# One head per 64-row matmul: splitting the product of v_m and w1 into two row halves, two banks and 32-partition evictions

## The chip, the cores and the metric

The kernel runs as one program on one core of a Trainium2 chip. The metric is the device time of one execution in microseconds (us); lower is better. The engines are named as the profile names them: PE (matmul), PEld (the weight loads of PE), DVE (VectorE), ACT (ScalarE), POOL (GpSimd) and SP (the queue that issues DMAs). A "column" of a matmul below is one column of its moving operand.

## What is computed

```python
# q, k, v: (8 batches, 8 heads, 576, 64); phi: (8, 8, 576, 32)
a = softmax(phi, axis=2)                       # over the 576 positions
k_m = einsum('bhsm,bhsd->bhmd', a, k)          # 32 memory rows per head
v_m = einsum('bhsm,bhsd->bhmd', a, v)
attn = softmax(q @ k_m.T / 8, axis=-1)         # over the 32 memory rows
x = concat_heads(attn @ v_m)                   # (4608, 512)
p = domain_probs / domain_probs.sum(-1)        # (4608, 4)
for e in range(4):                             # w1[e]: 512 x 1024, w2[e]: 1024 x 512
    out += p[:, e:e+1] * (relu(x @ w1[e]) @ w2[e])
```

## The kernel before

**The folding.** `x @ w1` is never formed from `x`. Since `x` is `attn @ v_m`, the kernel first multiplies each head's `v_m` (32 x 64) by that head's 64 rows of `w1`; this product is called `vw`. Then the first expert product takes `vw` and the transposed attention `AT`, and contracts over 8 heads x 32 memory rows = 256 instead of 512.

**Numbers.** Nearly every operand is held as a high part, rounded to fp32r, and a low part that is the rest. A product is three matmuls: high by high, high by low, low by high. So every eviction from PSUM that makes such an operand is a pair: ACT copies (and thereby rounds) the high part, then DVE subtracts it from the PSUM value for the low part.

**The stages.** The eight batches are taken as four pairs `k`; each pair has `PAIR = 128` steps, 32 for each of the four experts `e`. A step `s` stands for one batch of the pair (`odd`), one half of its 576 positions and one `j` of the eight 128-wide slices of the 1024 hidden columns. In step `s` the loop at L628 to L631 does three things: it runs the units that a plan has put at `s`, it issues `first(s + 2)` and it issues `second(s)`.

- `first` (L405) makes six matmuls (L415 to L417, twice) of 256 or 320 columns into a tile `p1`, then the relu on ACT (L427) and the low part on DVE (L429) into `h`, and for the wide halves into `hm` too.
- `second` (L434) makes six matmuls of 512 columns (L445 to L447, twice; nine where the middle tile is due) into `p2` tiles, and at the last `j` adds them into `acc` on DVE (L460, L462).

**The part that is changed.** `vw_unit` (L392) makes `vw` for one pair of heads `hp` and one half `fh` of the hidden columns. It calls `vw_mm` (L361): three matmuls of 512 columns (L364 to L366) into one PSUM tile `pv` of 128 partitions x 512. The stationary operand is `vt`, written by `write_vt` (L281): its 128 rows are the 64 dimensions of the two heads of the pair, its 128 columns are four blocks of 32 (two batches x two heads), and it is zero where row and column are not of the same head. So one product gives both heads of both batches. `vw_out` (L369) then evicts, for each batch in `odds`, 64 partitions: one ACT copy (L379) and one DVE subtraction (L380).

**Where the units stand.** The eight units of an expert are planned in the steps 26 to 33 (`VW_AT`) counted from the start of the expert before it, one in each step, both batches each. There are 15 such windows. The first expert of the first pair is made apart: four units by `vw_mm` in the prologue, which the change doesn't touch, four units for the even batch and eight for the odd batch within the first 18 steps, one batch each. That makes 120 + 12 = 132 units by `vw_unit`. Beside the units, the same windows hold the splits of the next expert's weights (L118 on ACT, L119 on DVE).

**PSUM and the order of work.** There are eight PSUM tiles: four with the tag `p2` for the sums of `second`, and four with the tag `pm`, which everything else takes in turn: `p1`, `pv` and the tiles of the attention. A tile with the tag `pm` can be taken again once all reads of the tile four allocations earlier are done. After the prologue, which is scheduled by hand, a scheduler puts the instructions of each engine into one fixed order; each engine then runs its list in that order and waits where an operand isn't there.

Of the kernel before, what the change touches and what calls it, by code (L numbers as in the profile page):

```python
# [28 lines left out]
F32 = mybir.dt.float32  # L29
F32R = mybir.dt.float32r  # L30
# [5 lines left out]
B, H, S, D, M = 8, 8, 576, 64, 32  # L36
N, DM, E, F = 4608, 512, 4, 1024
P = 128
# [31 lines left out]
def body(ctx: ExitStack, tc: tile.TileContext, qm, qt, kv, kvt, phi, prob, w1, w2, out):  # L70
    nc = tc.nc
    pool = lambda name, **k: ctx.enter_context(tc.tile_pool(name=name, bufs=1, **k))
    const, wp, work, att = pool("const"), pool("wp"), pool("work"), pool("att")
    psum = pool("psum", space=PSUM)
# [40 lines left out]
    w1t, w2t = {}, {}  # L115
# [25 lines left out]
    st = {}  # L141
# [217 lines left out]
    vw = {}  # L359

    def vw_mm(k, fh, hp, tag):  # L361
        vt, w = st["vt", k], w1t[fh, hp]
        ps = psum.tile([P, 512], F32, name="pv", tag=tag[0], bufs=tag[1])
        nc.tensor.matmul(ps, vt[:, hp, 0, :], w[:, 0, :], start=True, stop=False)  # L364
        nc.tensor.matmul(ps, vt[:, hp, 0, :], w[:, 1, :], start=False, stop=False)  # L365
        nc.tensor.matmul(ps, vt[:, hp, 1, :], w[:, 0, :], start=False, stop=True)  # L366
        return ps

    def vw_out(ps, fh, hp, odds):  # L369
        g = hp // 2  # L370
        for odd in odds:
            if hp % 2 == 0:
                vw[odd, fh, g] = att.tile(
                    [P, 2, 512], F32R, name="vw", tag=f"vw{odd}", bufs=4 + odd
                )
            q = (hp % 2) ^ odd
            r = slice(64 * q, 64 * q + 64)
            t = vw[odd, fh, g]
            nc.scalar.copy(t[r, 0, :], ps[r])  # L379
            nc.vector.tensor_sub(t[r, 1, :], ps[r], t[r, 0, :].bitcast(F32))  # L380
# [9 lines left out]
        nc.gpsimd.tensor_sub(t[r, 1, :], tmp[r, 0, :], t[r, 0, :].bitcast(F32))  # L390

    def vw_unit(k, e, fh, hp, odds, tag):  # L392
        vw_out(vw_mm(k, fh, hp, tag), fh, hp, odds)


    hs, mid, acc, po = {}, {}, {}, {}
# [83 lines left out]
    def vw_at(s, *a):  # L480
        at(s, lambda: vw_unit(*a, ("pm", 4)))

    rest = [unit_scores(0, t0) for t0 in (2, 4)] + [lambda t0=t0: transposes(0, t0) for t0 in (2, 4)]
    rest += [unit_w1(0, 0, 1, g) for g in range(2)]
    rest += [unit_w2(0, 0, j2) for j2 in range(1, 4)]
    rest += [lambda hp=hp: vw_unit(0, 0, 1, hp, (0,), ("pm", 4)) for hp in range(NP)]
    for s, u in zip(REST_0, rest):
        at(s, u)
# [9 lines left out]
    for k in range(NG):  # L498
        for e in range(E):
            s = k * PAIR + e * STEPS  # L500
            nk, ne = (k, e + 1) if e + 1 < E else (k + 1, 0)
            if nk < NG:
                for j2 in range(4):
                    at(s + W2_AT[j2], unit_w2(nk, ne, j2))
                n = 0
# [6 lines left out]
        if k + 1 < NG:  # L512
            b = 2 * k + 2
# [37 lines left out]
    with tc.manual_schedule():  # L551
# [45 lines left out]
        q = raw["qm", 0, 0]  # L597
# [9 lines left out]
        for i in range(2):  # L607
            t = wp.tile([P, 2, DM], F32R, name="w2", tag="w2", bufs=NJ + 2)
# [3 lines left out]
        for i in range(2):  # L612
            t = w2t[0, 0, i]
            dve.tensor_sub(t[:, 1, :], raw["w2", 0, 0][:, i, :], t[:, 0, :].bitcast(F32))
        pv = [vw_mm(0, 0, hp, ("p2", 4)) for hp in range(4)]
# [52 lines left out]
```

## Time and profile before

| what | value |
|---|---|
| time, median of 2 runs | 1426.86 us (1426.07 to 1427.65) |
| time of the profiled execution | 1428.84 us |
| its span, first to last instruction | 1427.1 us |
| PE busy | 1412.3 us (99%), 7808 matmuls |
| PEld busy | 1233.5 us (86%) |
| DVE busy | 837.2 us (59%), 1853 instructions |
| ACT busy | 620.2 us (43%), 1543 instructions |
| POOL busy | 27.8 us (2%) |
| mean granted TensorE clock | 0.996 |

How to read it: a matmul's listed duration runs from its start to its modelled end, and matmuls overlap, so a 512-column matmul that lasts 0.39 us in the list can be followed by the next one 0.23 us later. What a matmul costs is the distance from its start to the start of the next. DVE and ACT instructions that follow each other without a wait overlap a little as well. Idle time of an engine that nothing waits for costs nothing.

### The profile page before, as it was taken

Reading aid. Unit: us, or ns where it says so; the run is one execution under the profiler, and the core shown is the slowest. Engines: PE = TensorE matmul, PEld = TensorE weight load, DVE = VectorE, ACT = ScalarE, POOL = GpSimd, SP = SyncE. Lnnn points to the kernel's source line nnn. Section 1 sums busy time; section 2 is a strip of 40 time slices with the busy share of each in tenths; the row PEclk is TensorE's granted clock in tenths of the full one; section 3 lists DMA queues with packets and bytes.
Section 4 is the critical chain, followed back from the end, with each engine's and each line's share of the span. In section 5 each row is a group of like instructions: output and inputs, shape, how many; then the busy total and the mean of one; then the engine's idle time right before and its main releaser. Section 6 shows DMA issues by size and latency. Waiting matters only on the chain.

```text
span 1427.1 us, 20830 instructions
## 1 busy us (share of the span) xinstructions
PE 1412.3 (99%) x7808; PEld 1233.5 (86%) x7808; DVE 837.2 (59%) x1853; ACT 620.2 (43%) x1543; POOL 27.8 (2%) x27
## 2 busy tenths in 40 slices
PE   7999999999999999999999999999999999999998
PEld 6888888888888888888888888888888888888887
DVE  7876638666385654837547375573846446272722
ACT  6655426453263533635335362452625234161521
POOL 3300000000000000000000000000000000000000
PEclk8999999999999999999999999999999999999999
DMA  6632303323141120412214121140323103030001
GB/s 245 198 118 75 121 28 126 104 64 104 39 161 61 64 89 16 137 58 78 94 63 135 59 88 65 46 130 18 107 75 96 60 25 94 1 119 1 1 30 38
DMA packets 35957, 115.20 MB, mean 81 GB/s; under 512 B 3984, under 2 KB 5136, under 8 KB 35856
## 3 DMA queue, kind: packets, MB, share of 16 engines
q1 hardware_dynamic: 35856, 113.86, 24.5%
q8 instruction: 62, 1.02, 0.3%
q14 instruction: 39, 0.32, 0.1%
HBM read 104.41 MB, written 9.44 MB: 80 GB/s over the span
## 4 chain that ended last, share of the span: by engine, by line
PE 92%; DMA 2%; DVE 2%; ACT 2%; issue 1%; POOL 0%; SPq 0%; ACTq 0%
PE p L446 18%; PE p L447 18%; PE p L445 18%; PE p L415 9%; PE p L417 9%; PE p L416 9%; PE sc L304 2%; PE pv L366 2%; PE pv L364 2%; PE x L230 2%; PE pv L365 2%; DMA stage<-in_w 1%; PE tp L349 1%; PE kvp L249 1%; ACT w L118 0%
## 5 line engine op out<-in xcount | busy, mean ns | idle before, releaser
L446 PE MATMUL p<-w,h 128*128 128x512 f32 x1024 | 404.3, 395 | 0.0
L447 PE MATMUL p<-w,h 128*128 128x512 f32 x1024 | 402.8, 394 | 0.0
L445 PE MATMUL p<-w,h 128*128 128x512 f32 x1024 | 402.7, 393 | 0.0
L427 ACT ACTIVATE h<-p 128x256 fp32r<-128x256 f32 x512 | 195.2, 382 | 331.5 <-PE p L417 294.3
L429 DVE SCALAR_TENSOR_TENSOR h<-p,h 128x256 fp32r<-128x256 f32 x512 | 213.9, 418 | 206.3 <-ACT h L427 110.0
L415 PE MATMUL p<-AT,vw 128*128 128x256 f32 (+1 forms) x1024 | 308.2, 301 | 0.0
L417 PE MATMUL p<-AT,vw 128*128 128x256 f32 (+1 forms) x1024 | 304.3, 297 | 0.1
L416 PE MATMUL p<-AT,vw 128*128 128x256 f32 (+1 forms) x1024 | 303.6, 297 | 0.0
L447 PEld LDWEIGHTS p<-w,h 128*128 128x128 f32 x1024 | 192.4, 188 | 43.3 <-DVE nm L154 0.2
L119 DVE TENSOR_TENSOR w<-stage,w 128x512 fp32r<-128x512 f32 x259 | 175.9, 687 | 78.4 <-ACT w L118 77.1
L445 PEld LDWEIGHTS p<-w,h 128*128 128x128 f32 x1024 | 193.2, 189 | 23.3
L446 PEld LDWEIGHTS p<-w,h 128*128 128x128 f32 x1024 | 192.6, 188 | 22.0
L416 PEld LDWEIGHTS p<-AT,vw 128*128 128x128 f32 x1024 | 194.5, 190 | 19.5 <-DVE AT L356 0.3
L415 PEld LDWEIGHTS p<-AT,vw 128*128 128x128 f32 x1024 | 194.0, 189 | 19.1
L417 PEld LDWEIGHTS p<-AT,vw 128*128 128x128 f32 x1024 | 193.5, 189 | 0.7 <-DVE vw L380 0.6
L118 ACT CAST w<-stage 128x512 fp32r<-128x512 f32 x262 | 159.6, 620 | 79.1 <-DMA stage<-in_w 47.3
L380 DVE TENSOR_TENSOR vw<-pv,vw 64x512 fp32r<-64x512 f32 x254 | 172.1, 685 | 8.9 <-ACT vw L379 5.5
L429 DVE SCALAR_TENSOR_TENSOR hm<-p,hm 128x64 fp32r<-128x64 f32 x256 | 56.0, 219 | 201.9 <-ACT h L427 200.9
L379 ACT CAST vw<-pv 64x512 fp32r<-64x512 f32 x254 | 145.5, 580 | 58.5 <-DVE vw L380 42.6
L427 ACT ACTIVATE hm<-p 128x64 fp32r<-128x64 f32 x256 | 56.6, 221 | 227.9 <-PE p L417 227.9
L462 DVE SCALAR_TENSOR_TENSOR acc<-p,pt,acc 128x512 f32<-128x512 f32 x96 | 67.8, 741 | 2.6 <-PE p L447 2.6
L366 PE MATMUL pv<-w,vt 128*128 128x512 f32 x136 | 53.7, 395 | 0.0
(81 smaller groups left out, 1020.5 us busy)
## 6 DMA issues: line engine op xcount, KB each, us to landing
stage<-in_w SPq DMA_DIRECT2D x132, 512.0 KB, 3.8
stage<-in_kv SPq DMA_DIRECT2D x32, 512.0 KB, 4.1
stage<-in_qm SPq DMA_DIRECT2D x16, 512.0 KB, 3.7
out<-acc SPq DMA_DIRECT2D x32, 256.0 KB, 2.1
ph<-in_phi SPq DMA_DIRECT2D x16, 288.0 KB, 3.5
stage<-in_kvt SPq DMA_DIRECT2D x8, 512.0 KB, 3.8
stage<-in_qt SPq DMA_DIRECT2D x8, 128.0 KB, 3.2
out<-accm SPq DMA_DIRECT2D x4, 256.0 KB, 2.2
```

Source lines behind the costliest of these rows:

```text
L118: nc.scalar.copy(dst[:, 0, :], raw)
L119: eng.tensor_sub(dst[:, 1, :], raw, dst[:, 0, :].bitcast(F32))
L379: nc.scalar.copy(t[r, 0, :], ps[r])
L380: nc.vector.tensor_sub(t[r, 1, :], ps[r], t[r, 0, :].bitcast(F32))
L415: nc.tensor.matmul(ps, w[:, 0, f], at_t[:, g, 0, c], start=g == 0, stop=False)
L416: nc.tensor.matmul(ps, w[:, 0, f], at_t[:, g, 1, c], start=False, stop=False)
L417: nc.tensor.matmul(ps, w[:, 1, f], at_t[:, g, 0, c], start=False, stop=g == 1)
L427: nc.scalar.activation(t[:, 0, to], ps[:, at_], AF.Relu)
L429: nc.vector.scalar_tensor_tensor(t[:, 1, to], ps[:, at_], 0.0, t[:, 0, to].bitcast(F32), ALU.max, ALU.subtract)
L445: nc.tensor.matmul(po[t], x[:, 0, :], w[:, 0, :], start=j == 0, stop=False)
L446: nc.tensor.matmul(po[t], x[:, 0, :], w[:, 1, :], start=False, stop=False)
L447: nc.tensor.matmul(po[t], x[:, 1, :], w[:, 0, :], start=False, stop=j == NJ - 1)
```

## The change

Only `vw_unit` changes. It takes two `pv` tiles with the tag `pm` in place of one. It makes six matmuls of 512 columns in place of three: for each of the three products, one with rows 0 to 63 of `vt` and `w1` into the first tile and one with rows 64 to 127 into the second. In the text they are issued in turn, first tile, second tile, first tile and so on. Each matmul still fills 128 output partitions, but only the 64 that belong to its head (32 for each batch) hold anything but zero. So the eviction of a batch becomes two pieces of 32 partitions x 512, one from each tile: two ACT copies and two DVE subtractions where there was one of each. The tiles `vw`, what reads them, and the four units of the prologue stay as they are. No DMA is added or moved.

```diff
     def vw_unit(k, e, fh, hp, odds, tag):
-        vw_out(vw_mm(k, fh, hp, tag), fh, hp, odds)
+        vt, w, g = st["vt", k], w1t[fh, hp], hp // 2
+        ps = [psum.tile([P, 512], F32, name="pv", tag=tag[0], bufs=tag[1]) for _ in range(2)]
+        for n, (a, b) in enumerate(((0, 0), (0, 1), (1, 0))):
+            for i in range(2):
+                r = slice(64 * i, 64 * i + 64)
+                nc.tensor.matmul(ps[i], vt[r, hp, a, :], w[r, b, :], start=n == 0, stop=n == 2)
+        for odd in odds:
+            if hp % 2 == 0:
+                vw[odd, fh, g] = att.tile(
+                    [P, 2, 512], F32R, name="vw", tag=f"vw{odd}", bufs=4 + odd
+                )
+            t = vw[odd, fh, g]
+            for i in range(2):
+                q = 64 * ((hp % 2) ^ odd) + M * i
+                r = slice(q, q + M)
+                nc.scalar.copy(t[r, 0, :], ps[i][r])
+                nc.vector.tensor_sub(t[r, 1, :], ps[i][r], t[r, 0, :].bitcast(F32))
```

The new lines move the rest of the file down by 16: L415 to L417 of `first` become L431 to L433, L429 becomes L445, L445 to L447 of `second` become L461 to L463, and L462 becomes L478.

The scheduler gives the new instructions places of its own. First PE, in the last window (the expert 3 of the last pair). Before, a step reads like this; `pv` is the unit's tile, `p1` is the tile of `first`, `p2` those of `second`, and the number behind a name tells tiles apart:

```order
L364 MATMUL pv_13029<-w1_12977,vt_8160 128x512
L365 MATMUL pv_13029<-w1_12977,vt_8160 128x512
L366 MATMUL pv_13029<-w1_12977,vt_8160 128x512
L415 MATMUL p1_13045<-AT_10452,vw_12368 128x256
L416 MATMUL p1_13045<-AT_10452,vw_12368 128x256
L417 MATMUL p1_13045<-AT_10452,vw_12368 128x256
L415 MATMUL p1_13045<-AT_10452,vw_12428 128x256
L416 MATMUL p1_13045<-AT_10452,vw_12428 128x256
L417 MATMUL p1_13045<-AT_10452,vw_12428 128x256
L445 MATMUL p2_12935<-w2_12215,h_12990 128x512
L446 MATMUL p2_12935<-w2_12215,h_12990 128x512
```

In the changed kernel the same place of the window reads:

```order
L398 MATMUL pv_14013<-w1_13953,vt_8744 128x512 x3
L461 MATMUL p2_13903<-w2_13119,h_13966 128x512
L462 MATMUL p2_13903<-w2_13119,h_13966 128x512
L398 MATMUL pv_14014<-w1_13953,vt_8744 128x512 x3
L431 MATMUL p1_14037<-AT_11228,vw_13310 128x256
L432 MATMUL p1_14037<-AT_11228,vw_13310 128x256
L433 MATMUL p1_14037<-AT_11228,vw_13310 128x256
L431 MATMUL p1_14037<-AT_11228,vw_13386 128x256
L432 MATMUL p1_14037<-AT_11228,vw_13386 128x256
L433 MATMUL p1_14037<-AT_11228,vw_13386 128x256
L463 MATMUL p2_13903<-w2_13119,h_13966 128x512
L461 MATMUL p2_13907<-w2_13119,h_13966 128x512
```

The two heads (`pv_14013` and `pv_14014`) no longer take turns: the three matmuls of the one stand together, other matmuls of 128 rows come between, and the three of the other follow just ahead of `p1`. Counted over the whole list, the 792 new matmuls stand in 222 separate groups, 182 of them of three matmuls of one head. In every one of the 15 windows two units keep their six matmuls in turn (six neighbouring pairs) and the other six units are split like the one shown, 14 groups in all.

Second, DVE at the same place. Before, from one relu remainder `h` to the next (`w1` and `w2` are splits of weights):

```order
L429 SCALAR_TENSOR_TENSOR h_13020<-p1_13013,h_13020 128x256
L119 TENSOR_TENSOR w1_13042<-stage_12917,w1_13042 128x512
L380 TENSOR_TENSOR vw_12974<-pv_13005,vw_12974 64x512
L119 TENSOR_TENSOR w2_12948<-stage_12371,w2_12948 128x512
L380 TENSOR_TENSOR vw_13033<-pv_13029,vw_13033 64x512
L429 SCALAR_TENSOR_TENSOR h_13052<-p1_13045,h_13052 128x256
```

And in the changed kernel, from one `h` to the next:

```order
L445 SCALAR_TENSOR_TENSOR h_14004<-p1_13997,h_14004 128x256
L409 TENSOR_TENSOR vw_13948<-pv_13981,vw_13948 32x512
L119 TENSOR_TENSOR w2_13916<-stage_13315,w2_13916 128x512
L409 TENSOR_TENSOR vw_13948<-pv_13982,vw_13948 32x512
L409 TENSOR_TENSOR vw_14021<-pv_14013,vw_14021 32x512
L409 TENSOR_TENSOR vw_14021<-pv_14014,vw_14021 32x512
L119 TENSOR_TENSOR w1_14034<-stage_13885,w1_14034 128x512
L119 TENSOR_TENSOR w2_13975<-stage_13855,w2_13975 128x512
L409 TENSOR_TENSOR vw_14026<-pv_14013,vw_14026 32x512
L409 TENSOR_TENSOR vw_14026<-pv_14014,vw_14026 32x512
L119 TENSOR_TENSOR w2_13978<-stage_13855,w2_13978 128x512
L445 SCALAR_TENSOR_TENSOR h_14044<-p1_14037,h_14044 128x256
```

Between two `h` there are now up to six evictions of `vw` where there were two; the splits of weights stay among them.

## The prediction

> **What bounds the kernel now.** I read the chain that ended last first, since it says which engine sets the end (shares of the span by engine):
>
> ```profile
> PE 92%; DMA 2%; DVE 2%; ACT 2%; issue 1%; POOL 0%; SPq 0%; ACTq 0%
> ```
>
> PE holds 92% of the chain. It is fed all the time, so whatever is added to PE's list is added to the time, unless it can run beside something. The list of who waited for whom says how little the `vw` work holds PE up today (engine, line, waited for: us in total, times, longest):
>
> ```profile
> ACT vw L379 <- DVE vw L380: 42.6, 64, 1.6
> ...
> PEld p L417 <- DVE vw L380: 0.6, 1, 0.6
> ```
>
> ACT waits 42.6 us for DVE inside the evictions, PE 0.6 us for their end. Then I looked at the windows in which the units stand, 23 us each, because a share over the whole span hides them. Columns: window, its length, then busy us of PE, PEld, DVE, ACT, POOL with counts, granted clock, DMA. The last row is a stretch between two windows; the sum is over 14 of the 15 windows.
>
> ```profile
> 1169.00:1192.00 23.00, 23.00 (x127) 19.97 (x126) 21.93 (x38) 20.01 (x39) 0.00 (x0) 1.00 0.42 127
> 1250.00:1273.00 23.00, 23.00 (x127) 19.93 (x127) 21.86 (x38) 20.05 (x39) 0.00 (x0) 1.00 0.41 126
> ...
> sum 322.00, PE 322.00 PEld 278.88 DVE 298.50 ACT 258.79 POOL 0.00; mean PE 23.00 PEld 19.92 DVE 21.32 ACT 18.49 POOL 0.00
> ```
> ```profile
> 1111.00:1169.00 58.00, 58.00 (x308) 50.71 (x307) 19.38 (x52) 11.72 (x42) 0.00 (x0) 1.00 0.07 22
> ```
>
> In a window DVE works 21.3 of 23 us; between windows 19.4 of 58. So DVE, at 59% of the span, is nearly full exactly where the change adds to it, and PE is full everywhere. The clock is 1.00 in these rows; it has no part in what follows.
>
> **PE: the added matmuls.** A 512-column matmul of the unit, start to start:
>
> ```profile
> 1333.47 0.39 PE L447 MATMUL p<-w,h 128*128 128x512 f32 x1
> 1333.69 0.39 PE L364 MATMUL pv<-w,vt 128*128 128x512 f32 x1
> 1333.92 0.39 PE L365 MATMUL pv<-w,vt 128*128 128x512 f32 x1
> 1334.15 0.40 PE L366 MATMUL pv<-w,vt 128*128 128x512 f32 x1
> 1334.38 0.28 PE L415 MATMUL p<-AT,vw 128*128 128x256 f32 x1
> ```
>
> Each takes 0.23 us of PE. The 132 units make 396 matmuls now and 792 after. A matmul of 64 rows streams the same 512 columns, so I take 0.23 us for each too. A window has 8 units: 24 more matmuls, +5.5 us. Two matmuls might run at the same time when they are neighbours and use different halves, but the order leaves few such: six pairs in a window, worth at most 6 x 0.23 = 1.4 us. In the six split units the neighbours use the same half, or all 128 rows.
>
> **PE: going in and out of 64-row work.** The trace has 64-row matmuls, the last transposes of `AT`. I compare them with the 128-row transposes, both between the same lines:
>
> ```profile
> 711.40 0.39 PE L447 MATMUL p<-w,h 128*128 128x512 f32 x1
> 711.72 0.34 PE L349 MATMUL tp<-ident,at 64*128 64x64 f32 x2
> 711.99 0.41 PE L415 MATMUL p<-AT,vw 128*128 128x320 f32 x1
> 712.24 0.31 PE L416 MATMUL p<-AT,vw 128*128 128x320 f32 x1
> ```
> ```profile
> 708.70 0.39 PE L447 MATMUL p<-w,h 128*128 128x512 f32 x1
> 708.93 0.60 PE L349 MATMUL tp<-ident,at 128*128 128x128 f32 x4
> 709.28 0.39 PE L415 MATMUL p<-AT,vw 128*128 128x320 f32 x1
> 709.51 0.31 PE L416 MATMUL p<-AT,vw 128*128 128x320 f32 x1
> ...
> ```
> ```profile
> L349 PE MATMUL tp<-ident,at 128*128 128x128 f32 x64 | 9.7, 275 | 2.1 <-DVE at L329 2.0
> ```
>
> Going in: 711.72 - 711.40 = 0.32 us against 0.23. For the round trip I go from L447 to L416: 0.84 us with two 64-row transposes, 0.81 us with four 128-row ones. One transpose step is (0.60 - 0.275) / 3 = 0.11 us, so two 128-row ones would give 0.81 - 0.22 = 0.59 us: the excursion costs 0.25 us. The bounds are 0.09 us (only the entry is paid, the way back hidden) and 0.25 us; I take 0.25, the nearest row, a whole excursion between the same neighbours. A window has 14 excursions: +3.5 us. PE's work in a window then comes to 23.0 + 5.5 + 3.5 = 32.0 us, or 30.6 us if neighbouring pairs overlap.
>
> The Trainium skill, in "TensorE: Matmul & The Clock Gate", section "Part 3: Packing small matmuls — row/col tiling", says that matmuls of few rows on different row groups run concurrently, starting some 4 ns apart. No row here shows two neighbours in different halves. By that page the pairs that stand side by side overlap, which gives the 30.6 us; without it the 32.0 us.
>
> **DVE and ACT: the added evictions.** One instruction of each kind (busy, mean ns):
>
> ```profile
> L119 DVE TENSOR_TENSOR w<-stage,w 128x512 fp32r<-128x512 f32 x259 | 175.9, 687 | 78.4 <-ACT w L118 77.1
> L380 DVE TENSOR_TENSOR vw<-pv,vw 64x512 fp32r<-64x512 f32 x254 | 172.1, 685 | 8.9 <-ACT vw L379 5.5
> ...
> L379 ACT CAST vw<-pv 64x512 fp32r<-64x512 f32 x254 | 145.5, 580 | 58.5 <-DVE vw L380 42.6
> ```
>
> The same 512 columns on 128 partitions take 687 ns and on 64 take 685 ns, so 32 partitions will take about as long and the work doubles in instructions: 252 more on each engine. When nothing is waited for, DVE's instructions overlap; start to start in a full window:
>
> ```profile
> 1255.52 0.68 DVE L119 TENSOR_TENSOR w<-stage,w 128x512 fp32r<-128x512 f32 x1
> 1256.12 0.68 DVE L380 TENSOR_TENSOR vw<-pv,vw 64x512 fp32r<-64x512 f32 x1
> 1256.72 0.68 DVE L119 TENSOR_TENSOR w<-stage,w 128x512 fp32r<-128x512 f32 x1
> 1257.31 0.68 DVE L380 TENSOR_TENSOR vw<-pv,vw 64x512 fp32r<-64x512 f32 x1
> ```
>
> That is 0.60 us each, the lower bound, and 0.69 us the upper. A window gets 16 more: +9.6 to +11.0 us, so DVE needs 30.9 to 32.3 us. ACT gets 16 more of at most 0.58 us: 18.5 + 9.3 = 27.8 us, not the bound. Unlike today DVE has no room left to hide these in a 23 us window. It has in the 58 us behind it, but only for work that nothing near waits for, such as the weight splits.
>
> **The waits that this adds.** Two tiles for a unit instead of one means that of the four `pm` tiles the second `pv` of a unit needs the first `pv` of the unit before to be fully evicted (two ACT and two DVE pieces), and the `p1` behind it needs the second. If such a tile is late, PE stands before the second group of three, and all of `first` and `second` in its list stand behind it; the `h` of that step is late next. The price is unknown, since PE doesn't wait for this today. Lower bound 0: the pieces of one unit end while PE does the 6 matmuls of `second` and 6 of `first`. Upper bound: in each of the six split units one whole pair of pieces, 0.58 + 0.69 = 1.27 us, so 7.6 us in a window. I take 1 us, near the lower bound, since the order puts each second group as late as it can go; a gain isn't possible, a tile isn't free earlier than before.
>
> **The sum.** PE (32.0) and DVE (30.9 to 32.3) end a window together, and 1 us of waits gives 33.0: +10 us in each of 15 windows, +150 us. The twelve early units make 36 more matmuls (8.3 us) in 13 excursions (3.3 us), less up to 24 pairs (5.5 us) if neighbours overlap: 6 to 12 us, I take 10. The span goes from 1427.1 to 1587 us. The profiled execution took 1428.84 us, 1.7 over its span; the median of the runs shown is 1426.86, 0.2 below that span, so I forecast **1587 us**, +11%.
>
> **The rivals.**
>
> *Pairs overlap and DVE catches up behind the window.* Then PE alone counts: 30.6 - 23 = 7.6 us a window, +114 us, and 6 us early: **1547 us**. For it: DVE is one-third busy in the 58 us between windows. Against it: the evictions themselves gate the next `first`, and they are the larger half of DVE's list. It needs both the overlap and the catching up. Chance 0.25. The page of the Trainium skill named above speaks for the overlap.
>
> *The four `pm` tiles decide.* Each second group waits for half a pair of pieces more than I took: 6 x 0.64 = 3.8 us on top of 33, so +13.8 us a window and 10 early: **1644 us**. For it: ACT already waits 64 times for DVE within one tile's evictions, and DVE is full. Against it: the second tile's pieces can fill the gaps of the first. Chance 0.27.
>
> *Not slower.* A 64-row matmul takes half the time, 0.115 us, as it fills half of the array, and of an excursion only the entry is paid, 0.09 us. The place is the same groups on PE: 792 x 0.115 + 222 x 0.09 = 111 us where 396 x 0.23 = 91 us stood, +20 us, so **1447 us**, within 2% (28.5 us, about what a measurement of this kernel can tell from no change). It decides from the point where matmuls and excursions together stay under 91 + 28.5 = 120 us, and needs DVE's 9.6 us a window to be carried out of the windows. Against it: two 64-row transposes and the way back take 0.27 us, no less than 128-row ones, and the evictions gate the next `first`. Chance 0.03.
>
> **How the numbers follow.** The forecast holds 0.45 (1565 to 1612), the overlap 0.25 (1525 to 1565), the tiles 0.27 (1612 to 1700), not slower 0.03. The range takes in the first, more than half of the second and about two-thirds of the third: **1538 to 1655 us**. Only the last case isn't slower by over 2%: faster 0.01, within 2% 0.02, slower 0.97.
>
> **What would show it.** Right: a window of eight units lasts 32 to 34 us, DVE busy over 30 of it; L398 starts 0.23 us apart in a group of three; the matmul behind a group starts about 0.1 us late, as does the first of the group; the 32-partition pieces last 0.68 and 0.58 us; between windows nothing changes. Wrong: a window of 30 us or less (DVE isn't a bound), PE waits of over 4 us a window on `vw` (the tiles decide), or L398 under 0.15 us apart within a group of three.

## The result, and the profile after

| | before | with the change |
|---|---|---|
| time, median | 1426.86 us | 1594.3 us (1593.49 to 1595.12, 2 runs) |
| ratio | 1 | 1.117 (95% interval 1.113 to 1.122) |
| span of the profiled execution | 1427.1 us | 1593.3 us |
| matmuls; DVE; ACT instructions | 7808; 1853; 1543 | 8204; 2105; 1795 |

The forecast was 1587 us, range 1538 to 1655. First the chain that ended last (shares of the span), and the groups of the changed line on PE, DVE and ACT (busy us, mean ns, idle before):

```profile
PE 94%; DMA 3%; DVE 2%; ACT 1%; issue 0%; POOL 0%; SPq 0%; ACTq 0%; POOLq 0%
...
L409 DVE TENSOR_TENSOR vw<-pv,vw 32x512 fp32r<-32x512 f32 x504 | 345.8, 686 | 30.2 <-ACT vw L408 17.9
...
L408 ACT CAST vw<-pv 32x512 fp32r<-32x512 f32 x504 | 286.6, 576 | 89.2 <-PE pv L398 80.6
...
L398 PE MATMUL pv<-w,vt 64*128 64x512 f32 x792 | 221.3, 428 | 0.2 <-DVE vw L409 0.2
```

PE still makes the chain. A piece of 32 partitions takes 686 ns on DVE and 576 on ACT, as long as one of 64 took (685 and 580). By the list, PE stood idle for only 0.2 us in all before the 792 matmuls.

The windows, from the table by stretches, now 35 us long (columns as before: PE, PEld, DVE, ACT, POOL, clock, DMA). The sum is over 14 windows:

```profile
1304.00:1339.00 35.00, 34.98 (x159) 23.22 (x158) 31.45 (x50) 29.66 (x55) 0.00 (x0) 1.00 0.23 76
1395.00:1430.00 35.00, 34.98 (x159) 23.18 (x159) 31.17 (x50) 29.48 (x55) 0.00 (x0) 1.00 0.24 76
...
sum 490.00, PE 489.73 PEld 325.36 DVE 441.46 ACT 390.71 POOL 0.00; mean PE 34.98 PEld 23.24 DVE 31.53 ACT 27.91 POOL 0.00
```

The length of one expert is read from where its window starts. In the last pair of batches, where no attention is made between the windows, these are the first `pv` matmuls of the last two windows, first before the change and then with it:

```profile
1249.84 0.39 PE L364 MATMUL pv<-w,vt 128*128 128x512 f32 x1
...
1330.91 0.39 PE L364 MATMUL pv<-w,vt 128*128 128x512 f32 x1
```
```profile
1395.08 0.97 PE L398 MATMUL pv<-w,vt 64*128 64x512 f32 x6
...
1486.36 0.97 PE L398 MATMUL pv<-w,vt 64*128 64x512 f32 x6
```

So one expert takes 91.3 us in place of 81.1: +10.2 us. From the first to the last `pv` matmul a window takes 32.3 us where it took 20.0, and the stretch to the next window 59.0 us where it took 61.1, since 52 in place of 42 matmuls of `second` are now issued inside the window. Over all 14 distances from window to window the mean grows by 10.4 us, and the start of the first window moves from 122.0 to 131.8 us. Fifteen experts at +10.2 and these 9.8 us are 163 of the 166 us.

What an excursion into 64-row work looks like on PE, from the timeline (start, duration, engine, line):

```profile
1486.05 0.39 PE L463 MATMUL p<-w,h 128*128 128x512 f32 x1
1486.36 0.97 PE L398 MATMUL pv<-w,vt 64*128 64x512 f32 x6
1487.26 0.38 PE L431 MATMUL p<-AT,vw 128*128 128x256 f32 x1
1487.48 0.28 PE L432 MATMUL p<-AT,vw 128*128 128x256 f32 x1
...
1493.00 0.39 PE L463 MATMUL p<-w,h 128*128 128x512 f32 x1
1493.32 0.96 PE L398 MATMUL pv<-w,vt 64*128 64x512 f32 x3
1494.21 0.50 PE L461 MATMUL p<-w,h 128*128 128x512 f32 x1
1494.54 0.40 PE L462 MATMUL p<-w,h 128*128 128x512 f32 x1
1494.87 0.96 PE L398 MATMUL pv<-w,vt 64*128 64x512 f32 x3
1495.76 0.39 PE L431 MATMUL p<-AT,vw 128*128 128x256 f32 x1
1495.99 0.28 PE L432 MATMUL p<-AT,vw 128*128 128x256 f32 x1
```

By an excursion I mean one stretch of 64-row matmuls between 128-row ones, way in and way out together. Two things stand here. The six matmuls of two heads in turn (1486.36 to 1487.26) take 0.90 us, the three of one head (1493.32 to 1494.21) 0.89 us: neighbours in different halves run at the same time, and the second head is free. In the whole trace 99 of the 792 start within 20 ns of the one before, 3 ns behind it at the median. Second, an excursion is paid four times: the first matmul comes 0.32 us after its neighbour in place of 0.23, three matmuls take 0.89 in place of 3 x 0.23 = 0.69, the first 128-row one is followed after 0.33 in place of 0.23 (1494.21 to 1494.54), and of the 0.20 too much inside, half is the way out. The sum is 0.09 + 0.20 + 0.10 = 0.39 us. The weight loads show where the second and fourth part come from. Within 128-row work PEld starts the next load together with the matmul ahead. At a change the first load starts only with its own matmul, the next load 0.11 us behind it, and the second matmul is late by as much.

```profile
1493.32 0.52 PEld L398 LDWEIGHTS pv<-w,vt 64*128 64x128 f32 x3 [0.35 <-issue]
...
1495.76 0.19 PEld L431 LDWEIGHTS p<-AT,vw 128*128 128x128 f32 x1 [0.36 <-issue]
...
1495.87 0.19 PEld L432 LDWEIGHTS p<-AT,vw 128*128 128x128 f32 x1
```

Not every pair that stands side by side starts together. The second unit of each window reads like this:

```profile
1398.25 1.30 PE L398 MATMUL pv<-w,vt 64*128 64x512 f32 x6
1399.48 0.50 PE L461 MATMUL p<-w,h 128*128 128x512 f32 x1
```

It takes 1.23 us in place of 0.90: the second tile's first matmul comes 0.34 us after the first tile's, and only two of its three pairs start together. So five of a window's six pairs overlap, 1.1 us. Counted in the trace, 14 of the 15 windows have 14 excursions, the second window has 13 and the early units have 13, which makes the 222.

The Trainium skill, "TensorE: Matmul & The Clock Gate", section "Part 3: Packing small matmuls — row/col tiling", has matmuls on different row groups start about 4 ns apart; the trace agrees, with 3 ns at the median, where the two matmuls are neighbours and the second tile is free, which holds for 99 of 396 pairs.

### The profile page after: what moved, and what is told of

Read it like the earlier page. It is cut to its first block, busy times and chain, and to the rows that moved or that the text cites. A ratio compares the mean times of both kernels' runs of the same rounds, so it can differ in the third digit from the quotient of the medians.

```text
span 1593.3 us, 22215 instructions
## 1 busy us (share of the span) xinstructions
PE 1574.8 (99%) x8204; PEld 1260.5 (79%) x8204; DVE 1026.4 (64%) x2105; ACT 771.2 (48%) x1795; POOL 27.2 (2%) x27
## 4 chain that ended last, share of the span: by engine, by line
PE 94%; DMA 3%; DVE 2%; ACT 1%; issue 0%; POOL 0%; SPq 0%; ACTq 0%; POOLq 0%
PE p L463 17%; PE p L461 17%; PE p L462 16%; PE pv L398 12%; PE p L431 10%; PE p L432 8%; PE p L433 8%; PE sc L304 2%; PE x L230 2%; DMA stage<-in_w 1%; PE tp L349 1%; PE kvp L249 1%; DMA stage<-in_kv 0%; DMA ph<-in_phi 0%; DMA stage<-in_kvt 0%
## 5 line engine op out<-in xcount | busy, mean ns | idle before, releaser
L461 PE MATMUL p<-w,h 128*128 128x512 f32 x1024 | 407.9, 398 | 0.2 <-ACT h L443 0.2
L462 PE MATMUL p<-w,h 128*128 128x512 f32 x1024 | 403.5, 394 | 0.0
L463 PE MATMUL p<-w,h 128*128 128x512 f32 x1024 | 402.1, 400 | 0.4 <-DVE h L445 0.4
L409 DVE TENSOR_TENSOR vw<-pv,vw 32x512 fp32r<-32x512 f32 x504 | 345.8, 686 | 30.2 <-ACT vw L408 17.9
L445 DVE SCALAR_TENSOR_TENSOR h<-p,h 128x256 fp32r<-128x256 f32 x512 | 214.7, 420 | 186.8 <-ACT h L443 94.4
L408 ACT CAST vw<-pv 32x512 fp32r<-32x512 f32 x504 | 286.6, 576 | 89.2 <-PE pv L398 80.6
L431 PE MATMUL p<-AT,vw 128*128 128x256 f32 (+1 forms) x1024 | 320.5, 313 | 1.2 <-DVE vw L409 0.9
L433 PE MATMUL p<-AT,vw 128*128 128x256 f32 (+1 forms) x1024 | 302.9, 296 | 0.2 <-DVE vw L409 0.2
L432 PE MATMUL p<-AT,vw 128*128 128x256 f32 (+1 forms) x1024 | 303.0, 296 | 0.0
L431 PEld LDWEIGHTS p<-AT,vw 128*128 128x128 f32 x1024 | 193.4, 189 | 60.2 <-issue 43.7
L463 PEld LDWEIGHTS p<-w,h 128*128 128x128 f32 x1024 | 188.9, 188 | 58.8 <-issue 22.2
L461 PEld LDWEIGHTS p<-w,h 128*128 128x128 f32 x1024 | 192.6, 188 | 44.0 <-ACT vw L408 9.9
L398 PE MATMUL pv<-w,vt 64*128 64x512 f32 x792 | 221.3, 428 | 0.2 <-DVE vw L409 0.2
L462 PEld LDWEIGHTS p<-w,h 128*128 128x128 f32 x1024 | 192.6, 188 | 23.1
L433 PEld LDWEIGHTS p<-AT,vw 128*128 128x128 f32 x1024 | 193.1, 189 | 1.3 <-DVE vw L409 0.4
L445 DVE SCALAR_TENSOR_TENSOR hm<-p,hm 128x64 fp32r<-128x64 f32 x256 | 55.8, 218 | 201.4 <-ACT h L443 200.1
L398 PEld LDWEIGHTS pv<-w,vt 64*128 64x128 f32 x792 | 111.3, 184 | 80.5 <-issue 38.2
```

The lines of the kernel that those rows point to most:

```text
L398: nc.tensor.matmul(ps[i], vt[r, hp, a, :], w[r, b, :], start=n == 0, stop=n == 2)
L408: nc.scalar.copy(t[r, 0, :], ps[i][r])
L409: nc.vector.tensor_sub(t[r, 1, :], ps[i][r], t[r, 0, :].bitcast(F32))
L431: nc.tensor.matmul(ps, w[:, 0, f], at_t[:, g, 0, c], start=g == 0, stop=False)
L432: nc.tensor.matmul(ps, w[:, 0, f], at_t[:, g, 1, c], start=False, stop=False)
L433: nc.tensor.matmul(ps, w[:, 1, f], at_t[:, g, 0, c], start=False, stop=g == 1)
```

## The experiments

The theory after the first look: PE alone sets the time, by the unit prices of the gaps (0.231 us a matmul, 0.227 us back for a pair side by side, 0.39 us an excursion), and the evictions just fit beside it. It is called theory A in the expectations. Its rival, theory B, is the forecast's own terms: no overlap, 0.25 us an excursion, DVE as full as PE. All ratios are against runs of the kernel before on the same chip.

### e1: both halves, one eviction

```diff
-            for i in range(2):
-                q = 64 * ((hp % 2) ^ odd) + M * i
-                r = slice(q, q + M)
-                nc.scalar.copy(t[r, 0, :], ps[i][r])
-                nc.vector.tensor_sub(t[r, 1, :], ps[i][r], t[r, 0, :].bitcast(F32))
+            q = 64 * ((hp % 2) ^ odd)
+            r = slice(q, q + 64)
+            nc.scalar.copy(t[r, 0, :], ps[0][r])
+            nc.vector.tensor_sub(t[r, 1, :], ps[0][r], t[r, 0, :].bitcast(F32))
```

> The six 64-row matmuls into two tiles as in the change, but only the first tile is evicted, in one piece of 64 partitions, so the second head of each pair is left out of vw and DVE and ACT have their old load. The program order then keeps all 396 pairs side by side, in 128 excursions into 64-row work. Theory A (only PE counts: 0.231 us for an added matmul, 0.227 us back for a pair side by side, 0.39 us for an excursion, as the changed kernel's gaps read): 1427 + 91.5 - 90 + 50 = 1478 us. Theory B (as forecast: no overlap, 0.25 us an excursion): 1427 + 91.5 + 32 = 1550 us. Overlap with 0.25 us an excursion: 1460 us.

Measured: 1485.0 us, ratio 1.040 (1.039 to 1.042). Near theory A's 1478, far from 1550 without overlap and above the 1460 of overlap with 0.25 us. In the trace 393 of the 792 matmuls start within 20 ns of the one before. So 396 matmuls were added and nearly none of them is paid for, though here DVE and ACT have only their old load.

### e2: one half alone

```diff
-        vw_out(vw_mm(k, fh, hp, tag), fh, hp, odds)
+        vt, w = st["vt", k], w1t[fh, hp]
+        ps = psum.tile([P, 512], F32, name="pv", tag=tag[0], bufs=tag[1])
+        for n, (a, b) in enumerate(((0, 0), (0, 1), (1, 0))):
+            r = slice(0, 64)
+            nc.tensor.matmul(ps, vt[r, hp, a, :], w[r, b, :], start=n == 0, stop=n == 2)
+        vw_out(ps, fh, hp, odds)
```

> Three matmuls of rows 0 to 63 alone into one tile, evicted as before the change; the second head's half of the product is left out. As many matmuls as before the change, so what is added is 128 excursions and nothing else. At 0.39 us each (theory A): 1477 us. At 0.25 us (theory B): 1459 us. At 0.18 us (only the late first and the late following matmul): 1450 us. If the second half of e1 is quite free, the two times are equal.

Measured: 1474.0 us, ratio 1.033 (1.031 to 1.034). Its span is 1472.4 us, 45.3 over the 1427.1 of before, for 128 excursions: 0.354 us each. This is the disputed price by itself, against 0.25 in the forecast. The gaps gave 0.39, and between the last two windows the trace gives the same:

```profile
1289.05 0.96 PE L397 MATMUL pv<-w,vt 64*128 64x512 f32 x3
...
1373.23 0.96 PE L397 MATMUL pv<-w,vt 64*128 64x512 f32 x3
```

That is 84.2 us where 81.1 stood, 3.1 us for eight excursions, 0.39 each. So 0.39 is the price of an excursion; 0.354 is what is left of it over the whole span, because PE's other gaps got about 5 us shorter than before. The other half costs 11 us more (e1), of which PE waits for `h` account for 7 us:

```profile
PE p L430 <- DVE h L444: 7.3, 10, 1.2
```

### e11: the same with two units to a step

```diff
-                            vw_at(s + VW_AT + n, nk, ne, fh, 2 * g + i, (0, 1))
+                            vw_at(s + VW_AT + n // 2 * 2, nk, ne, fh, 2 * g + i, (0, 1))
```

> One row half alone, as in the run that measured 1474 us, with the units planned two to a step, so that the program order has 68 excursions of mostly six matmuls in place of 128 of three. If the price is one of entering and leaving 64-row work: 1427 + 68 x 0.354 = 1451 us. If it is one of each 64-row matmul (45 us / 384 = 0.118 us): 1474 us as before.

Measured: 1452.7 us, ratio 1.018 (1.016 to 1.020). As many 64-row matmuls as in e2, about half the excursions, and (1451.0 - 1427.1) / 68 = 0.351 us for each; between the last two windows it is 82.65 - 81.07 = 1.58 us for four, 0.395 each, as in e2. So the price belongs to going in and out, not to the 64-row matmul.

### e3: the pieces alone

The edit is in the changed kernel's `vw_unit`:

```diff
-        ps = [psum.tile([P, 512], F32, name="pv", tag=tag[0], bufs=tag[1]) for _ in range(2)]
-        for n, (a, b) in enumerate(((0, 0), (0, 1), (1, 0))):
-            for i in range(2):
-                r = slice(64 * i, 64 * i + 64)
-                nc.tensor.matmul(ps[i], vt[r, hp, a, :], w[r, b, :], start=n == 0, stop=n == 2)
+        ps = [vw_mm(k, fh, hp, tag)] * 2
```

> The three 128-row matmuls and one tile as before the change, evicted in the 32-partition pieces of the change: only DVE and ACT get more. Theory A (evictions are hidden as long as they fit beside PE) doesn't cover this one, since here a window's PE work is 23 us and DVE's about 31: if DVE can drain its list behind the window, about 1430 us; if each window lasts as long as DVE, 1427 + 15 x 8 = 1547 us. Theory B (DVE as large a bound as PE): 1547 us. I expect some of both, about 1480 us.

Measured: 1543.1 us, ratio 1.081 (1.079 to 1.083). PE has not one matmul more than before, and loses 116 us. That is near the 1547 us of windows that last as long as DVE's list, and far from the 1480 that I expected. The table by stretches for two of its windows, and who waited on PE:

```profile
1260.00:1288.00 28.00, 24.53 (x120) 18.69 (x119) 25.48 (x42) 24.91 (x48) 0.00 (x0) 1.00 0.28 95
1348.00:1376.00 28.00, 24.54 (x120) 18.72 (x119) 25.48 (x42) 24.91 (x48) 0.00 (x0) 1.00 0.29 94
```
```profile
PE pv L364 <- DVE h L441: 30.2, 19, 1.9
PE p L427 <- DVE vw L405: 13.5, 16, 1.5
```

PE stands 3.5 of 28 us, mostly before `pv` and `p1` matmuls, for tiles that DVE has not yet read. From one window to the next, in the last pair, it takes 88.0 us in place of 81.1, so a window loses 6.9 us, at a clock of 1.00. Part of the 116 us lies elsewhere: the mean granted clock of the whole run is 0.988 where it was 0.996, by my estimate at most 0.008 x 1540 = 12 us. Theory A, with evictions hidden, holds only as long as PE is slow enough: the evictions are a second bound, 116 us above the kernel before where the change is 167.

### e5 and e6: the weight splits moved from DVE to POOL

The same edit on e3's kernel (e5) and on the kernel before (e6, the control):

```diff
-                split_w1(raw, fh, 2 * g + i, nc.vector)
+                split_w1(raw, fh, 2 * g + i, nc.gpsimd)
...
-    def unit_w2(k, e, j2, eng=nc.vector):
+    def unit_w2(k, e, j2, eng=nc.gpsimd):
```

> The 32-partition pieces alone (128-row matmuls, one tile, 1543 us), with the weight splits' subtraction on POOL. A window's DVE work falls by the 8 to 10 splits it holds, 0.60 to 0.69 us each, from about 31 to about 25 us, near PE's 23. If DVE's load is what the pieces cost (theory B): 1427 + 15 x 2 = 1457 us or less. If it is something else about small pieces, such as the turns of ACT and DVE on one tile: still about 1540 us.

> The kernel before with the weight splits' subtraction on POOL and nothing else; the control for the two runs that move the splits. If POOL's slower splits (1.29 us for 0.69) do no harm: 1427 us, within 3 us. If they make weights late or slow DVE down: more, and what it is more by is to be taken off the other two.

Measured: e6 1445.6 us, ratio 1.013 (1.012 to 1.015), so moving the splits costs 19 us by itself; e5 1524.2 us, ratio 1.068 (1.066 to 1.070). Against its control the pieces still cost 79 us, where they cost 116. DVE is no longer full in a window:

```profile
1255.00:1283.00 28.00, 26.17 (x131) 20.14 (x130) 21.64 (x37) 26.36 (x51) 19.59 (x16) 1.00 0.40 132
```

So by these times DVE's load is about a third of what the pieces cost, 37 of 116 us. The two edits may not simply add up: in e5 PE also waits 18.5 us for ACT's copies of `xs` in the attention, against 1.4 in e6. The last pair has no attention to make and is the cleaner place: from window to window it takes 81.1 us before and in e6, 88.0 in e3 and 85.0 in e5, so there moving the splits takes off 3.0 of 6.9 us. Either way, theory B, that DVE's load is the price, falls for the larger part.

What remains is not settled. One candidate is how long a tile is held. From the start of a unit's last matmul to the end of its last DVE read it is 4.0 us before, 8.7 in e3 and 8.0 in e5 (medians over the units of the windows, taken in order). Another is ACT, which is now the fuller of the two, at 26.4 of 28 us; no run takes work off ACT, so this stays untested.

### e10: copies first

```diff
-            for i in range(2):
-                q = 64 * ((hp % 2) ^ odd) + M * i
-                r = slice(q, q + M)
-                nc.scalar.copy(t[r, 0, :], ps[i][r])
-                nc.vector.tensor_sub(t[r, 1, :], ps[i][r], t[r, 0, :].bitcast(F32))
+        todo = [(vw[odd, fh, hp // 2], slice(q, q + M)) for odd in odds
+                for q in (64 * ((hp % 2) ^ odd), 64 * ((hp % 2) ^ odd) + M)]
+        for t, r in todo:
+            nc.scalar.copy(t[r, 0, :], ps[0][r])
+        for t, r in todo:
+            nc.vector.tensor_sub(t[r, 1, :], ps[0][r], t[r, 0, :].bitcast(F32))
```

> The pieces alone on one tile (1543 us), with all of a unit's ACT copies issued before its DVE subtractions; the same instructions, fewer turns between ACT and DVE on the tile (1 in place of 4). Moving the weight splits off DVE took 19 us of 116, or 37 us against its own control, so load on DVE is not the whole price. If the turns are the rest: about 1490 us. If not: 1543 us.

Measured: 1595.2 us, ratio 1.118 (1.117 to 1.120): 52 us worse than e3, which neither 1490 nor 1543 foresaw. Giving up the turns between ACT and DVE saves nothing here, and PE waits for the last subtractions:

```profile
PE pv L364 <- DVE vw L405: 34.1, 61, 0.8
PE p L427 <- DVE vw L405: 22.1, 22, 1.5
```
```profile
1400.00:1432.00 32.00, 25.74 (x121) 19.14 (x120) 30.38 (x50) 25.16 (x48) 0.00 (x0) 0.95 0.21 66
```

The run doesn't price the turns by themselves, since more than the turns changed: DVE is full in this window, at 30.4 of 32 us, and the granted clock there is 0.95 (0.980 over the run, where e3 has 0.988). It does say that holding time alone isn't the price: a tile is held for 7.2 us here, less than the 8.7 of e3, and the run is longer.

### e9: two tiles, all rows

```diff
-                r = slice(64 * i, 64 * i + 64)
-                nc.tensor.matmul(ps[i], vt[r, hp, a, :], w[r, b, :], start=n == 0, stop=n == 2)
+                nc.tensor.matmul(ps[i], vt[:, hp, a, :], w[:, b, :], start=n == 0, stop=n == 2)
```

> The change with all 128 rows in each of its six matmuls, so that both tiles hold both heads; tiles, pieces and the order on every engine stay exactly as in the change. What goes is the 64-row work itself: 222 excursions at 0.354 us, and 99 overlaps at 0.227 us come back as full matmuls. Theory A: 1594.3 - 78.6 + 22.5 = 1538 us, so faster than the change with the same number of matmuls. If 64-row work pays for itself: 1594 us or more. If DVE's list alone sets the windows: 1594 us too.

Measured: 1579.0 us, ratio 1.107 (1.105 to 1.109). The order on every engine is that of the change, so only the 64-row work differs. By the unit prices PE's list got 56 us shorter (78.6 - 22.5); the time fell by 15. In place of the excursions PE now waits: after the first 100 us its `pv` matmuls start 49 us late in all (against 0.231 us behind a 512-column matmul), and their weight loads wait most for the `h` that frees the tile. DVE's share of the window has hardly moved:

```profile
PEld pv L397 <- DVE h L444: 44.7, 104, 1.0
```
```profile
1289.00:1324.00 35.00, 33.79 (x168) 26.14 (x167) 32.14 (x52) 30.36 (x56) 0.00 (x0) 1.00 0.22 76
```

Theory A alone is refuted here: the evictions hardly delay the change, but they stand directly behind PE. It also says that the row halves, which were to be the point of the change, are worth less than nothing in this order: the same six matmuls over all 128 rows are 1% faster (1579.0 against 1594.3 us).

### e7: one head after the other

```diff
-        for n, (a, b) in enumerate(((0, 0), (0, 1), (1, 0))):
-            for i in range(2):
-                r = slice(64 * i, 64 * i + 64)
+        for i in range(2):
+            r = slice(64 * i, 64 * i + 64)
+            for n, (a, b) in enumerate(((0, 0), (0, 1), (1, 0))):
                 nc.tensor.matmul(ps[i], vt[r, hp, a, :], w[r, b, :], start=n == 0, stop=n == 2)
```

> The change with the matmuls of a unit in another order of text, three of the first head and then three of the second; evictions and tiles as in the change. The program order then has 206 excursions and 61 places where the two heads' matmuls are neighbours (changed kernel: 222 and 115). With the unit prices of the runs so far (0.231 a matmul, 0.354 an excursion, 0.227 back for a pair, about 10 us of waits): 1427 + 91.5 + 73 - 14 + 10 = 1587 us. If the overlap counted for nothing and excursions 0.25: 1594 - 4 = 1590 us. If DVE alone set the windows: 1594 us. Little tells these apart in the time; the trace does: 0.23 us between matmuls of one head, near 0 at the one place where the head changes.

Measured: 1597.5 us, ratio 1.120 (1.118 to 1.122). 10 us over theory A's sum and 3 over the change: 16 excursions fewer bring nothing. In the trace 85 starts lie within 20 ns of the one before, more than the 61 changes of head that I counted in the order. The run doesn't tell the theories apart.

### e4, e8 and e12: three ways to keep the pairs together

e4 is the change with e5's edit. In e8 each matmul of a unit is pinned behind the one before:

```diff
-            for i in range(2):
+            for i in (1, 0):
                 r = slice(64 * i, 64 * i + 64)
-                nc.tensor.matmul(ps[i], vt[r, hp, a, :], w[r, b, :], start=n == 0, stop=n == 2)
+                mm = nc.tensor.matmul(ps[i], vt[r, hp, a, :], w[r, b, :], start=n == 0, stop=n == 2)
+                if (n, i) != (0, 1):
+                    tc.keep_in_program_order(mm)
```

In e12 every `tag="pm", bufs=4` reads `bufs=5` and every `tag="p2", bufs=4` reads `bufs=3`.

> The change, with the weight splits' subtraction moved from DVE to POOL, which is idle: DVE has room in the windows, and the program order then keeps 302 pairs side by side in 148 excursions (changed kernel: 115 and 222). Theory A: 1427 + 91.5 - 302 x 0.227 + 148 x 0.39 = 1508 us. If it's DVE's load itself that costs, and pairs and excursions little: window shorter by DVE's 6 us, about 1594 - 90 = 1504 us too, but then without overlapping starts in the trace. If neither counts: 1594 us. Risk: POOL's 1.29 us for a split makes weights late.

> The change with each of a unit's six matmuls pinned behind the one before it on PE, second tile first, to keep heads in turn. The program order then has 306 pairs side by side and 223 excursions, 91 of them of a single matmul. Theory A with the prices so far: 1427 + 91.5 - 306 x 0.227 + 223 x 0.354 = 1528 us if nothing waits. If DVE's list of about 31 us a window (1543 us with the pieces alone) is a floor of its own: not under 1543 us. If pinned matmuls wait for the second tile in front of all else: 1560 us or more.

> The change with five pm tiles and three p2 tiles in place of four and four. The program order then keeps 297 pairs side by side in 136 excursions. If the lack of a free second tile is what parts the heads: 1427 + 91.5 - 67.4 + 48.1 = 1499 us, plus what second() now waits for its third tile (64 halves, at most one 0.74 us sum each, 47 us): 1499 to 1546 us. If DVE's list is a floor of its own as in the pieces alone: not under 1543 us.

Measured: e4 1570.0 us, ratio 1.101 (1.099 to 1.103); e8 1578.5, ratio 1.107 (1.105 to 1.108); e12 1562.9, ratio 1.096 (1.094 to 1.098). By the unit prices PE's added list is 144 us in the change (91.5 - 115 x 0.227 + 222 x 0.354) and 75, 101 and 72 us in these three, so 43 to 72 us shorter; the time got 16 to 31 us shorter (e4 also carries the 19 us of e6). All three are better than the change, all are over theory A's sums (1508, 1528, 1499 to 1546 us), and none comes under e3's 1543 us: part of what PE gains goes into waits for tiles. Of the 302, 306 and 297 pairs that stand side by side in the order, 210, 249 and 178 start together in the trace; the rest fits a second tile that isn't free when the first is. In e12 PE stands before `p1`:

```profile
PE p L431 <- DVE h L445: 15.7, 20, 0.9
PE p L431 <- DVE vw L409: 12.2, 26, 0.8
```

No version beat the kernel before, and by these prices none of this kind can: a pair side by side takes as long as the one 128-row matmul that it replaces (three pairs 0.90 us, part of the excursion included, three 128-row matmuls 0.69), and the excursion comes on top.

## Why the prediction was right

**The size.** Forecast 1587 us, measured 1594. For one expert +10 us was forecast and +10.2 measured in the last pair; for the early part +10 and +9.8. PE's list makes nearly all of it, as forecast: 91.5 us of added matmuls, 222 x 0.39 = 86.6 of excursions, less 99 x 0.227 = 22.5 of overlap, are 156 of the 166 us. That it comes within 7 us is partly luck, since three terms were off and cancel, as the next paragraphs show.

**What bounds it.** PE and DVE were said to end a window together, DVE with 30.9 to 32.3 us. DVE works 31.5 us of a 35 us window, and e3 and e9 show the two bounds from both sides: with no PE work added the pieces alone give 1543 us, and with the 64-row price taken off PE the time falls by 15 of 56 us. In the change itself PE is the one that ends last: it is idle for 0.02 us of a 35 us window.

**The matmuls.** 0.23 us each, +5.5 us a window, holds within a group of three from its second matmul on. The sum took nothing off for overlap. That was wrong: five of the six neighbouring pairs of a window do run together, and 1.1 us of the 5.5 are not paid. The overlap rival named this rightly. Its other half, that PE alone counts, also fits the change, where PE's waits for tiles come to 0.3 us a window. It came out at 1547 us because it priced the excursion at 0.25 too; and with a PE list that short DVE would have held PE back, as e9 shows (1579 where PE's list alone gave 1538). So the forecast's joint end of PE and DVE is near the truth and not quite it: PE ends the window, with DVE close behind.

**The excursion.** This is the term that was mis-sized: 0.25 us was taken, 0.39 is what e2 and e11 measure between windows (0.354 and 0.351 net over the span), so 14 cost 5.5 us a window in place of 3.5. The row that I read, the transposes, was another kind of work. Its 128-row side is sound: 0.23 us, four steps of 0.11 and 0.15 make the 0.81 that was read. On its 64-row side the first transpose is 0.09 us late and the second expert matmul 0.10, as in the change. But the two transposes with their way out take 711.99 - 711.72 = 0.27 us, only 0.05 more than two steps of 0.11, where three matmuls of the unit take 0.20 more than 0.69. So 0.25, called the bound from above, was no bound.

**The waits.** 1 us a window was taken for tiles. What is left in a window of the last pair after matmuls, overlap and excursions is 10.2 - 5.5 + 1.1 - 5.5 = 0.3 us, and the trace has it in one place, the late second tile of the window's second unit. So the sum had 1.1 us too much for the overlap, 0.7 too much for the waits and 2.0 too little for the excursions. The rival in which the four `pm` tiles decide would have had each second group wait: that did not come about.

**The signs.** The window, 32.3 us, and DVE's 31.5 us in it came as named, and so did the late matmuls on the way in and out. Two did not: between windows the stretch did change, from 61.1 to 59.0 us, and in a group of three the second matmul starts 0.34 us after the first.

**What was not foreseen.** The reason why the pieces cost what they do alone: the forecast put it down to DVE's load, and moving the splits away took 37 of 116 us, or 3.0 of 6.9 in a window. PE's waits in e3, e5 and e12 point at when the `pm` tiles come free, but e10 holds them for a shorter time than e3 and is slower. Which of holding time, ACT's load and the clock makes the rest stays open.

## What to carry to other kernels

Row halves ran side by side at no cost only where their matmuls were neighbours in the order that runs and both tiles were free, and every stretch of 64-row work between 128-row work cost 0.39 us, way in and out together. So put many 64-row matmuls into one stretch, and count the stretches in the scheduled order, not in the text. Where the full-row matmul already held both heads by zeros, a pair wasn't faster than it. Evictions cost by their columns here, not by their partitions (686 ns for 32 partitions of 512 columns on DVE, 685 for 64): halving the partitions doubled DVE's and ACT's part, and that alone cost 116 us.

## What the runs showed of the hardware that I had not expected

The change between 128-row and 64-row matmuls is paid twice each way: the matmul that changes starts 0.09 us late, and the one behind it 0.10 us late, as its weight load starts that much late. The Trainium skill, "TensorEngine Tiling (Array Packing)", section "Tiling Modes", says that switching the mode drains the TensorE; the trace agrees in so far as the first matmul on each way starts 0.09 us late, and adds the late load. POOL's splits, though POOL was idle, cost the kernel before 19 us (e6): 4.5 us of it ahead of the first window and nearly all of the rest between the windows, where the attention of the next batches is made; in the last pair of batches, which has none to make, nothing is lost.
